# Attention scores in 64x64 quarters, router logits for two steps at once, and queries loaded half a pair per step, in a fused retention and mixture-of-experts kernel

## The chip, the cores and the metric

The kernel runs on one core of one Trainium2 chip. The time is device time in microseconds (us) of one execution on that core; of several runs the median counts, lower is better. A profile is taken from a run of its own, so its times belong to that one execution.

## What is computed

The reference has two stages. The first is a retention recurrence for 4 batches, 8 heads, 768 tokens and a head size of 64; the second routes each of the 3072 resulting rows to the best of 8 experts.

```python
gamma = 1.0 - 2.0 ** (-5.0 - np.arange(H, dtype=np.float32))
scale = 1.0 / np.sqrt(D)
for t in range(S):
    state = gamma[None, :, None, None] * state + np.einsum('bhd,bhe->bhde', k[:, :, t], v[:, :, t])
    y[:, :, t] = scale * np.einsum('bhd,bhde->bhe', q[:, :, t], state)
...
x = np.ascontiguousarray(attn_out.transpose(0, 2, 1, 3)).reshape(B * S, H * D)
...
logits = x @ w_gate
expert_idx = np.argmax(logits, axis=1)
...
    h = np.maximum(x_sorted[lo:hi] @ w1[e], 0.0)
    y_sorted[lo:hi] = h @ w2[e]
...
return (gate_w[:, None] * y).astype(np.float32)
```

`gate_w` is the softmax of the logits at the chosen expert. Everything is float32; x is 3072 x 512, w1 512 x 1024 and w2 1024 x 512 per expert.

## The kernel before

**Stages.** The attention comes first, in 12 steps, then the experts: 256 early tokens of expert 0, then all eight experts in a Strassen-like scheme of halves and quarters (from L1171 on), which is most of the time. The change is in the attention only.

**The steps.** The 768 tokens are cut into six chunks of 128. A step `s` does one chunk for two of the four batches; `where[s]` names the pair of chunks `m`, the pair of batches `b1` and the parity `e`. Steps 0, 1 are the two chunks of the first pair for the first two batches, steps 2, 3 the same for the other two batches, and so on. Both chunks of a pair share one load of `q` (token pairs interleaved), so `q` belongs to even steps and serves the odd step behind it; `k` and `v` are loaded for each step. The decay factors are folded into `q` and `v` on load, so that a step is made of plain products.

**What a step does,** in the names of the profile, for each of its two batches `b`:

- `load` (L588): L594 brings `q` (512 KB, 4 buffers), L598 `k` or `v` (256 KB, 8 buffers), all issued by SP on one DMA queue.
- `scale_q` (L601, row L606) and `scale_v` (L609, row L611) multiply by the decays, mostly on POOL, and give `qs` and `vs`.
- `turn_q` (L622) and `turn_k` (L632) transpose on PE (both row L617, `trq` and `trk`) into a PSUM bank each, which ACT copies to `qT` and `kT` (L636).
- `scores` (L642, matmul L649): per pair of heads two products of 64 x 128 keys and 64 x 128 queries, in two banks of the group `sc`; DVE multiplies by the causal mask (`am`, L653).
- `with_state` (L665, L672): y from the state so far. `next_state` (L675, L685): `new` = k v, added to the state on DVE.
- `within` (L693, L703): y from the masked scores; ACT copies the result to `xT` (2 buffers).
- `logits` (L726, L731) multiplies `xT` of the step before by the router's weights (`parts`), ACT copies that to `lgT`; `logits_of` (L737) transposes it back (L740, named `parts` too), and DVE reduces it to `lg` (L741).
- `to_rows` (L710, L714) turns `xT` of the step before on DVE into `xg` (3 buffers); `store` (L717, L721) has SP write it to `x_d` in four transfers.

PSUM has 4 banks for `sc` (scores, `trq`, `parts`), 2 for `tr` (`trk`, `new`) and 2 for `y`.

**Routing.** `place` (L747) runs after steps 5 and 9 and after the end. It finds each row's expert, counts (`ohs` L765 on DVE, `rk` L783 on PE) and sets where each row goes; it is cut into pieces, which the table `WHEN` (L896) drops into places of the steps behind. The first 256 rows of expert 0 are gathered for the early layer, `hp`, that follows step 11.

**What sets the order.** Each engine does its instructions in the order in which the code writes them: from L864 on the order of PE, ACT, POOL, DVE and SP is written by hand. The loop over steps (L902 to L977) writes, for a step s: the loads of step s + 3 (v is left off near the end), the scaling of `q` and `v` on POOL, scores, y from the state, logits of step s - 1, the turn of the next keys, the logits' transposes, the turn of the next queries if s is odd, the rows and the store of step s - 1, `new`, and `within`. SP is one line too: a load or store waits for everything before it on SP, and a store waits for its rows. SP gets the store of step 5 late, in step 7, between that step's loads of k and v. Step 8's `to_rows` needs the `xg` buffer that step 5's rows leave. The functions follow.

Of the kernel before, what the change touches and what calls it, by code (L numbers as in the profile page):

```python
# [21 lines left out]
P = 128  # L22
# [31 lines left out]
def kernel(  # L54
# [513 lines left out]
    with ExitStack() as actx:  # L568
# [32 lines left out]
        def scale_q(s, b, by=nc.gpsimd, parts=1):  # L601
            got = raw.pop(("q", s, b))
            qs = raw["qs", s, b] = att.tile([P, 2, H, D], F32, tag="qs", name="qs")
            for part in (ts(i, H // parts) for i in range(parts)):
                for e in range(2):
                    by.tensor_tensor(out=qs[:, e, part, :], in0=got[:, part, ts(e, D)], op=ALU.mult,  # L606
                                     in1=inner(dec[:, ts(2 * where[s][0] + e, H)][:, part], D))
# [24 lines left out]
        def turn_k(s, b):  # L632
            kT = att.tile([P, HP, P], F32, tag="kT", name="kT")
            tr = pairs_of("tr", 2, "trk")
            heads_first(raw["k", s, b], tr)
            nc.scalar.copy(out=kT, in_=tr)  # L636
            front[s, b] = kT
# [4 lines left out]
        def scores(s, b):  # L642
            kT, qT = front.pop((s, b)), q_of(s, b)
            sc = [pairs_of("sc", 4, "sc") for _ in range(2)]
            am = [att.tile([P, HP, P], F32, tag=f"am{j}", name=f"am{j}") for j in range(2)]
            for a in range(HP):
                for j in range(2):
                    r = ts(j, D)
                    nc.tensor.matmul(sc[j][:, a, :], lhsT=kT[r, a, :], rhs=qT[r, a, :], start=True, stop=True)  # L649

            def mask():
                for j in range(2):
                    nc.vector.tensor_tensor(out=am[j], in0=sc[j], in1=middle(causal[:, :], HP), op=ALU.mult)  # L653

            return am, mask
# [70 lines left out]
        def logits(s):  # L726
            bank = ps("sc", 4, "parts")
            parts = bank[:, 0 : 2 * P]
            m = P // DT
            for dt in range(DT):  # L730
                nc.tensor.matmul(parts[ts(dt, m), :], lhsT=wg[:, dt, :], start=True, stop=True,  # L731
                                 rhs=x[s][:, dt, :, :].rearrange("p b t -> p (b t)"))
            lgT = att.tile([P, 2 * P], F32, tag="lgT", name="lgT", bufs=1)
            nc.scalar.copy(out=lgT, in_=parts)
            return lgT, bank

        def logits_of(s, lgT, bank):  # L737
            tr = bank[:, 2 * P : 4 * P].rearrange("p (b t) -> p b t", b=2)
            for b in range(2):
                nc.tensor.transpose(tr[:, b, :], lgT[:, ts(b, P)], ident)  # L740
            return lambda: nc.vector.tensor_reduce(  # L741
                lg[:, 2 * s : 2 * s + 2, :], tr.rearrange("p b (a e) -> p b e a", a=DT)[:, :, 0:E, :], axis=AX.X,
                op=ALU.add)
# [124 lines left out]
        scale_q(0, 0, nc.vector, 2)  # L868
# [33 lines left out]
        for s in range(STEPS):  # L902
            if s + 3 < STEPS:
                if s % 2:
                    load_all("q", s + 3)
                load_all("k", s + 3)
                if s == 7:
                    store(5)
                if s + 4 < STEPS:
                    load_all("v", s + 3)  # L910
            if s % 2 and s + 1 < STEPS:
                scale_q(s + 1, 1)
            if s + 2 < STEPS:
                for b in range(2):
                    scale_v(s + 1, b)
            if s % 2 == 0 and s + 2 < STEPS:
                scale_q(s + 2, 0)
            if s in (1, 2):
                nc.gpsimd.memset(xs2[s % 2], 0.0)
            if s:  # L920
                am = [scores(s, b) for b in range(2)]
                am[0][1]()
                step(s, "m")
                if s + 2 != STEPS:
                    am[1][1]()
            y = outputs()
            if s + 1 == STEPS:
                logit = logits(s - 1)
                rows_in_order()
# [12 lines left out]
            if s:  # L942
                if s + 1 < STEPS:
                    logit = logits(s - 1)
                    ahead()
                reduce = logits_of(s - 1, *logit)
                step(s, "p")
                if s + 2 == STEPS:
                    am[1][1]()
                    for b in range(2):  # L950
                        scale_v(s + 1, b)
                if s + 1 < STEPS:
                    ahead_q()
                to_rows(s - 1)
# [14 lines left out]
            next_state(s)  # L969
            step(s, "b")  # L970
# [4 lines left out]
            if s == 0:  # L975
                ahead()
# [9 lines left out]
        def within_early(f):  # L986
            nonlocal ne, arm, src, far
            if f == 1:
                logits_of(STEPS - 1, *logit)()
# [21 lines left out]
        for f in range(FT):  # L1011
            layer1(EARLY, xTa, wa[0], hTa, f, (("sc", 4),), lambda: within_early(f))
            if f == 0:
                logit = logits(STEPS - 1)
# [282 lines left out]
```

## Time and profile before

| | |
|---|---|
| median of 3 runs | 439.09 us (439.05 to 440.54) |
| the profiled execution's own time | 442.87 us |
| its span in the profile | 441.2 us |
| instructions in the profile | 9756 |
| PE busy | 420.9 us (95% of the span), 3595 matmuls |
| DVE / POOL / ACT busy | 244.9 / 252.6 / 130.4 us |
| attention | 0 to about 118.7 us, where the row `hp` of the early layer starts |
| moved by DMA in all | 85.39 MB, mean 194 GB/s |

The span runs from the first to the last instruction that the profiler saw, so it is a little shorter than the time. In the profile's rows, PE is the matmul part of the tensor engine and PEld its weight loads, which overlap; DVE is the vector engine, ACT the scalar engine, POOL the GpSimd engine, SP the engine that only issues transfers, and SPq its DMA queue. A row of the timeline is the start, the busy time, the engine and the source line, what is written and read with its shape, how many instructions stand in it, and in brackets how long the first one waited and for what. A row of the chain of waits is start, length, and who held the chain. Forty digits in a row are the span in forty equal slices, each digit the busy tenths. A row of the windows is the stretch, its length, busy time and count for PE, PEld, DVE, ACT and POOL, then the granted PE clock, the DMA engines' mean busy share and their GB/s. A row of one line's instructions gives the least, middle and greatest nanoseconds of one and the stretch in which they lie.

### The profile page before, as it was taken

How to read it: one execution, taken by the hardware profiler on the slowest of the kernel's cores; microseconds unless marked ns; L12 is line 12 of the kernel's file. 1: busy time of each engine (PE TensorE's matmuls, PEld its weight loads, DVE VectorE, ACT ScalarE, POOL GpSimd, SP SyncE). 2: the span in 40 equal slices, each digit the busy share in tenths (PEclk: the TensorE clock that was granted, in tenths of full speed). 3: DMA queues.
4: the chain of work that ended last, by engine and by line, in shares of the span. 5: the costliest groups of instructions: out<-in, count | busy, mean ns of one | idle time of the engine just before them, and what ended most of it. 6: DMA issues, size and time to landing. Idle time of an engine off the chain costs nothing.

```text
span 441.2 us, 9756 instructions
## 1 busy us (share of the span) xinstructions
PE 420.9 (95%) x3595; PEld 385.7 (87%) x3595; DVE 244.9 (56%) x565; ACT 130.4 (30%) x293; POOL 252.6 (57%) x212
## 2 busy tenths in 40 slices
PE   7889989999999999999999999999999999999990
PEld 4778877887788858999999999999999999999680
DVE  4445577769779960444672674377178247544320
ACT  2355452553521212201322222031223213303330
POOL 4477254553338352989329926983992892585051
PEclk9999999999999999999999999999999999999997
DMA  9989999999991497643955694496599449222222
GB/s 196 237 199 205 237 203 218 219 229 222 285 337 45 127 402 244 216 149 94 385 131 161 245 277 95 125 377 158 165 316 244 116 142 348 57 84 52 49 74 75
DMA packets 122123, 85.39 MB, mean 194 GB/s; under 512 B 56970, under 2 KB 106122, under 8 KB 122000
## 3 DMA queue, kind: packets, MB, share of 16 engines
q1 hardware_dynamic: 116736, 71.34, 59.5%
q0 software_dynamic: 5120, 12.60, 8.6%
q8 instruction: 49, 0.80, 0.8%
q14 instruction: 74, 0.61, 0.5%
q10 hardware_dynamic: 144, 0.05, 0.1%
HBM read 60.88 MB, written 14.68 MB: 171 GB/s over the span
## 4 chain that ended last, share of the span: by engine, by line
PE 82%; DMA 5%; SPq 4%; DVE 4%; issue 2%; ACT 1%; another core or an unknown queue 0%; POOLq 0%; DVEq 0%; ACTq 0%
PE p L333 51%; PE p L233 6%; DMA k<-in_k_dram 4%; PE p L246 4%; PE hp L233 3%; PE sc L649 3%; PE y L703 3%; SPq L598 3%; PE p L474 2%; PE new L685 2%; PE trq L617 2%; PE y L672 1%; PE trk L617 1%; DVE xTa L217 1%; PE parts L731 1%
## 5 line engine op out<-in xcount | busy, mean ns | idle before, releaser
L337 DVE TENSOR_TENSOR q<-p,q 128x196 f32<-128x196 f32 (+5 forms) x72 | 24.0, 352 | 41.8 <-PE p L333 35.1
L653 DVE TENSOR_TENSOR am<-sc,causal 128x512 f32<-128x512 f32 x48 | 30.0, 683 | 20.5 <-PE sc L649 20.4
L522 POOL DMA_INDIRECT out_dram<-o,dst x26 | 25.9, 996 | 26.4 <-ACT o L1167 19.5
L611 POOL TENSOR_TENSOR vs<-v,dec 128x512 f32<-128x512 f32 x23 | 24.6, 1084 | 26.5 <-DMA v<-in_v_dram 25.0
L174 POOL DMA_INDIRECT xs<-x_d,src x28 | 30.8, 1099 | 13.9 <-issue 9.8
L333 PE MATMUL p<-t,w1t 128*128 128x196 f32 (+5 forms) x192 | 35.9, 330 | 0.0
L333 PE MATMUL p<-t,s 128*128 128x196 f32 (+5 forms) x192 | 35.8, 329 | 0.0
L333 PE MATMUL p<-g,w2t 128*128 128x216 f32 (+5 forms) x192 | 35.3, 337 | 0.0
L337 DVE TENSOR_TENSOR yT<-p,q 128x216 f32<-128x216 f32 (+5 forms) x36 | 13.0, 374 | 39.5 <-PE p L333 31.0
L333 PE MATMUL p<-g,z 128*128 128x196 f32 (+4 forms) x192 | 33.6, 328 | 0.0
L333 PEld LDWEIGHTS p<-g,w2t 128*128 128x128 f32 x192 | 33.4, 190 | 0.0
L606 POOL TENSOR_TENSOR qs<-q,dec 128x512 f32<-128x512 f32 x22 | 22.4, 1044 | 19.1 <-DMA q<-in_q_dram 16.7
L337 DVE TENSOR_TENSOR hT<-p,q 128x196 f32<-128x196 f32 (+5 forms) x72 | 24.2, 351 | 16.0 <-PE p L333 15.6
L333 PE MATMUL p<-hT,w2t 128*128 128x196 f32 (+4 forms) x192 | 32.6, 328 | 0.0
L333 PEld LDWEIGHTS p<-t,w1t 128*128 128x128 f32 x192 | 32.4, 190 | 0.2 <-DVE q L337 0.2
L333 PEld LDWEIGHTS p<-t,s 128*128 128x128 f32 x192 | 32.5, 190 | 0.0
L1251 POOL COPY turn_of<-t 128x1 f32<-128x1 f32 x6 | 1.1, 184 | 54.5 <-DVE t L318 54.5
L333 PEld LDWEIGHTS p<-g,z 128*128 128x128 f32 x192 | 31.9, 190 | 0.0
L333 PEld LDWEIGHTS p<-hT,w2t 128*128 128x128 f32 x192 | 31.7, 190 | 0.0
L649 PE MATMUL sc<-qT,kT 64*128 64x128 f32 x384 | 24.9, 279 | 2.3 <-ACT kT L636 2.3
L649 PEld LDWEIGHTS sc<-qT,kT 64*128 64x128 f32 x384 | 22.4, 188 | 4.4 <-ACT kT L636 3.0
L703 PE MATMUL y<-am,vs 128*64 128x128 f32 x384 | 24.1, 274 | 0.5 <-issue 0.3
(231 smaller groups left out, 886.1 us busy)
## 6 DMA issues: line engine op xcount, KB each, us to landing
w1t<-in_moe_w_dram SPq DMA_DIRECT2D x7, 2048.0 KB
w2t<-in_moe_w_dram SPq DMA_DIRECT2D x7, 2048.0 KB
k<-in_k_dram SPq DMA_DIRECT2D x24, 256.0 KB
v<-in_v_dram SPq DMA_DIRECT2D x24, 256.0 KB
x_d<-xg SPq DMA_DIRECT2D x48, 128.0 KB
xs<-xs SPq DMA_DIRECT2D x96, 64.0 KB
o<-o SPq DMA_DIRECT2D x96, 64.0 KB
q<-in_q_dram SPq DMA_DIRECT2D x11, 512.0 KB
```

What stands on the lines that cost most here:

```text
L174: nc.gpsimd.indirect_dma_start(out=xs[:, t, :], out_offset=None, in_=x_d[0:rows, :], in_offset=bass.IndirectOffsetOnAxis(ap=idx[:, t : t + ...
L233: nc.tensor.matmul(hp, lhsT=w1t[:, 0, dt, ts(f, P)], rhs=xT[:, dt, n0:n], start=(dt == 0), stop=(dt == DT - 1))
L246: nc.tensor.matmul(y[j * z : j * z + m, 0:c], lhsT=hT[:, f, t * P + r0 : t * P + r0 + m], rhs=w2t[:, 0, f, ts(j, c)], start=(i == 0), stop ...
L333: nc.tensor.matmul(columns(y, c), lhsT=a, rhs=b, start=start and i == 0, stop=i + 1 == len(terms), skip_group_check=True)
L337: nc.vector.tensor_tensor(out=to, in0=y, in1=plus, op=ALU.add)
L522: done = nc.gpsimd.indirect_dma_start(out=out[:, :], out_offset=bass.IndirectOffsetOnAxis(ap=idx[:, t : t + 1], axis=0), in_=o[:, t, :], i ...
L606: by.tensor_tensor(out=qs[:, e, part, :], in0=got[:, part, ts(e, D)], op=ALU.mult, in1=inner(dec[:, ts(2 * where[s][0] + e, H)][:, part], D))
L611: by.tensor_tensor(out=vs, in0=raw.pop(("v", s, b)), op=ALU.mult, in1=inner(dec[:, ts(NC + 2 * where[s][0] + where[s][2], H)], D))
L617: nc.tensor.transpose(tr[:, a, :], src[:, 2 * a : 2 * a + 2, :].rearrange("p h d -> p (h d)"), ident)
L649: nc.tensor.matmul(sc[j][:, a, :], lhsT=kT[r, a, :], rhs=qT[r, a, :], start=True, stop=True)
L653: nc.vector.tensor_tensor(out=am[j], in0=sc[j], in1=middle(causal[:, :], HP), op=ALU.mult)
L703: nc.tensor.matmul(place_of(y, b, a, j), lhsT=vs[:, 2 * a + j, :], rhs=am[b][0][j][:, a, :], start=alone, stop=True, skip_group_check=True)
```

## The change

Six things change, all in the attention.

1. `scores` makes each product of 64 x 128 keys as two of 64 x 64 keys, each to one half of the partitions of the bank. A batch's step has 16 matmuls in place of 8; the profile counts each float32 matmul as two rows, so a step of two batches goes from 32 rows to 64.
2. `logits` takes a list of steps. Step 1 does step 0's; from step 3 on an odd step does the logits of the two steps before it, in one bank, with one copy, four transposes into the same bank and one reduction over both; an even step does none. Step 11's own logits stay alone.
3. `turn_k` of the second batch goes to a bank of `sc` in place of `tr` when it is called for the turn of an odd step's keys, which is done in an even step.
4. SP loads `k` first in each step, then one of the two `q` of the next even step (the first in even steps, the second in odd ones), then `v`. Among the first loads, `wg` and the `v` of step 1 move behind.
5. POOL scales accordingly; in step 1 the second `q` of step 2 is scaled half by DVE and half by POOL, and one `v` of step 1 by DVE. The two memsets of `xs2` are in steps 2 and 3 in place of 1 and 2.
6. Step 1's keys are turned ahead of step 0's `within` instead of behind it, and `to_rows` of step 0 is written ahead of those scalings in step 1.

The first place is SP's line around the store of step 5 (`x_d`, the fifth row), before:

```order
L598 DMA k<-in_k_dram 128x8x64 x2
L598 DMA v<-in_v_dram 128x8x64 x2
L594 DMA q<-in_q_dram 128x8x128 x2
L598 DMA k<-in_k_dram 128x8x64 x2
L721 DMA x_d<-xg 32x8x128 x4
L598 DMA v<-in_v_dram 128x8x64 x2
```

And after the change:

```order
L598 DMA k<-in_k_dram 128x8x64 x2
L594 DMA q<-in_q_dram 128x8x128
L598 DMA v<-in_v_dram 128x8x64 x2
L598 DMA k<-in_k_dram 128x8x64 x2
L594 DMA q<-in_q_dram 128x8x128
L723 DMA x_d<-xg 32x8x128 x4
L598 DMA v<-in_v_dram 128x8x64 x2
```

One `q` now stands ahead of `v` in the step before and one behind `k` in step 7; the transfers ahead of the store are the same set.

The second place is PE in step 11, the last step (`tot` belongs to the routing), before:

```order
L649 MATMUL sc<-qT,kT 128x128 x16
L731 MATMUL parts<-xT,wg 32x256 x4
L672 MATMUL y<-qT,state_1863 64x128 x16
L740 MATMUL parts<-ident,lgT 128x128 x2
L841 LDWEIGHTS ones_b
L841 MATMUL tot<-acc,ones_b 128x2
```

And after:

```order
L650 MATMUL sc<-qT,kT 64x128 x32
L734 MATMUL parts<-xT,wg 32x256 x8
L674 MATMUL y<-qT,state_2013 64x128 x16
L744 MATMUL parts<-ident,lgT 128x128 x4
L845 LDWEIGHTS ones_b
L845 MATMUL tot<-acc,ones_b 128x2
```

The order counts each matmul once and names the shape of its output, 128 x 128 before and 64 x 128 now; the scores' rows double. So do the logits' rows, since they hold steps 9 and 10.

The third place is PE in step 2, an even one (the y at the top ends `within` of step 1), before:

```order
L703 MATMUL y<-am_356,vs 64x128
L649 MATMUL sc<-qT,kT 128x128 x16
L731 MATMUL parts<-xT,wg 32x256 x4
L617 MATMUL trk<-ident,k 128x128 x8
L740 MATMUL parts<-ident,lgT 128x128 x2
L685 MATMUL new<-vs,k 64x64 x16
```

And after, with the start of `within` as the last row:

```order
L705 MATMUL y<-am_368,vs 64x128
L650 MATMUL sc<-qT,kT 64x128 x32
L617 MATMUL trk<-ident,k 128x128 x8
L687 MATMUL new<-vs,k 64x64 x16
L705 MATMUL y<-am_535,vs 64x128
```

Both rows of `parts` have left the step, and the rest keeps its order.

The diff, cut to its core:

```diff
         def turn_k(s, b):
             kT = att.tile([P, HP, P], F32, tag="kT", name="kT")
-            tr = pairs_of("tr", 2, "trk")
+            tr = pairs_of("sc", 4, "trk") if s % 2 and b else pairs_of("tr", 2, "trk")
...
             for a in range(HP):
-                for j in range(2):
-                    r = ts(j, D)
-                    nc.tensor.matmul(sc[j][:, a, :], lhsT=kT[r, a, :], rhs=qT[r, a, :], start=True, stop=True)
+                for c in range(2):
+                    for j in range(2):
+                        r = ts(j, D)
+                        nc.tensor.matmul(sc[j][ts(c, D), a, :], lhsT=kT[r, a, ts(c, D)], rhs=qT[r, a, :],
+                                         start=True, stop=True)
...
-        def logits(s):
+        def logits(steps):
+            n = 2 * len(steps)
             bank = ps("sc", 4, "parts")
...
+            for i, s in enumerate(steps):
+                for dt in range(DT):
+                    nc.tensor.matmul(bank[ts(dt, m), ts(i, 2 * P)], lhsT=wg[:, dt, :], start=True, stop=True,
+                                     rhs=x[s][:, dt, :, :].rearrange("p b t -> p (b t)"))
+            lgT = att.tile([P, 4 * P], F32, tag="lgT", name="lgT", bufs=1)
+            nc.scalar.copy(out=lgT[:, 0 : n * P], in_=bank[:, 0 : n * P])
...
-        nc.sync.dma_start(wg[:, :, 0:E], w_gate.rearrange("(dt p) e -> p dt e", p=P))
         load_all("v", 0)
         load_all("k", 1)
-        load_all("v", 1)
+        nc.sync.dma_start(wg[:, :, 0:E], w_gate.rearrange("(dt p) e -> p dt e", p=P))
         load("q", 2, 0)
+        load_all("k", 2)
+        load("v", 1, 0)
         load("q", 2, 1)
-        load_all("k", 2)
+        load("v", 1, 1)
...
             if s + 3 < STEPS:
-                if s % 2:
-                    load_all("q", s + 3)
                 load_all("k", s + 3)
+                n = s + 4 - s % 2
+                if n < STEPS:
+                    load("q", n, s % 2)
                 if s == 7:
                     store(5)
...
                 if s + 1 < STEPS:
-                    logit = logits(s - 1)
+                    if s % 2:
+                        logit = logits([s - 1] if s == 1 else [s - 2, s - 1])
                     ahead()
-                reduce = logits_of(s - 1, *logit)
+                reduce = logits_of(*logit) if s % 2 else lambda: None
...
+                if s == 1:
+                    to_rows(0)
+                    scale_q(2, 1, (nc.vector, nc.gpsimd))
+                    scale_v(1, 1)
+                    for b in range(2):
+                        scale_v(2, b)
...
             next_state(s)
+            if s == 0:
+                ahead()
             step(s, "b")
...
             within(s, y, am, early_rows if s + 1 == STEPS else lambda: None)
-            if s == 0:
-                ahead()
```

More of the change, by code (lines that the diff above doesn't have):

```diff
@@ L599, in load, with scale_q @@
             raw[nm, s, b] = to
-        def scale_q(s, b, by=nc.gpsimd, parts=1):
+        def scale_q(s, b, by=(nc.gpsimd, nc.gpsimd), parts=1):
             got = raw.pop(("q", s, b))
@@ L605, in scale_q @@
                 for e in range(2):
-                    by.tensor_tensor(out=qs[:, e, part, :], in0=got[:, part, ts(e, D)], op=ALU.mult,
+                    by[e].tensor_tensor(out=qs[:, e, part, :], in0=got[:, part, ts(e, D)], op=ALU.mult,
                                      in1=inner(dec[:, ts(2 * where[s][0] + e, H)][:, part], D))
@@ L724, with logits_of @@
         early, wa = [], []
-        def logits(s):
+        def logits(steps):
+            n = 2 * len(steps)
             bank = ps("sc", 4, "parts")
-            parts = bank[:, 0 : 2 * P]
             m = P // DT
[L730 to L739, printed above, removed]
+            for i, s in enumerate(steps):
[4 more added lines that the diff above has]
+            nc.scalar.copy(out=lgT[:, 0 : n * P], in_=bank[:, 0 : n * P])
+            return steps, lgT, bank
+        def logits_of(steps, lgT, bank):
+            n = 2 * len(steps)
+            tr = bank[:, 0 : n * P].rearrange("p (b t) -> p b t", b=n)
+            for b in range(n):
                 nc.tensor.transpose(tr[:, b, :], lgT[:, ts(b, P)], ident)
             return lambda: nc.vector.tensor_reduce(
-                lg[:, 2 * s : 2 * s + 2, :], tr.rearrange("p b (a e) -> p b e a", a=DT)[:, :, 0:E, :], axis=AX.X,
-                op=ALU.add)
+                lg[:, 2 * steps[0] : 2 * steps[0] + n, :], tr.rearrange("p b (a e) -> p b e a", a=DT)[:, :, 0:E, :],
+                axis=AX.X, op=ALU.add)
         MOST_T = 2 * max(b - a for a, b in zip(NEXT, NEXT[1:]))
@@ L867 @@
         hTa = keep.tile([P, FT, EARLY], F32, tag="hTa", name="hTa")
-        scale_q(0, 0, nc.vector, 2)
+        scale_q(0, 0, (nc.vector, nc.vector), 2)
         scale_q(0, 1)
@@ L910 @@
                     load_all("v", s + 3)
-            if s % 2 and s + 1 < STEPS:
-                scale_q(s + 1, 1)
-            if s + 2 < STEPS:
+            if s == 0:
+                scale_q(2, 0)
+            elif 1 < s < STEPS - 2:
+                if s % 2:
+                    scale_q(s + 1, 1)
                 for b in range(2):
                     scale_v(s + 1, b)
-            if s % 2 == 0 and s + 2 < STEPS:
-                scale_q(s + 2, 0)
-            if s in (1, 2):
+                if s % 2 == 0:
+                    scale_q(s + 2, 0)
+            if s in (2, 3):
                 nc.gpsimd.memset(xs2[s % 2], 0.0)
@@ L925 @@
                     am[1][1]()
+                if s == 1:
+                    scale_v(1, 0, nc.vector)
             y = outputs()
             if s + 1 == STEPS:
-                logit = logits(s - 1)
+                logit = logits([s - 2, s - 1])
                 rows_in_order()
@@ L943 @@
                 if s + 1 < STEPS:
-                    logit = logits(s - 1)
+                    if s % 2:
+                        logit = logits([s - 1] if s == 1 else [s - 2, s - 1])
                     ahead()
-                reduce = logits_of(s - 1, *logit)
+                reduce = logits_of(*logit) if s % 2 else lambda: None
                 step(s, "p")
@@ L951 @@
                         scale_v(s + 1, b)
+                if s == 1:
+                    to_rows(0)
[3 more added lines that the diff above has]
+                        scale_v(2, b)
                 if s + 1 < STEPS:
                     ahead_q()
-                to_rows(s - 1)
+                if s > 1:
+                    to_rows(s - 1)
                 reduce()
@@ L969 @@
             next_state(s)
+            if s == 0:
+                ahead()
             step(s, "b")
@@ L988, in within_early @@
             if f == 1:
-                logits_of(STEPS - 1, *logit)()
+                logits_of(*logit)()
                 next(rest)
@@ L1013 @@
             if f == 0:
-                logit = logits(STEPS - 1)
+                logit = logits([STEPS - 1])
         hs = [att.tile([P, FH * P], F32, tag="k", name="he", bufs=8) for _ in range(4)]
```

## The prediction

> **What bounds the kernel now.** I began with the page, asked for the chain of waits over the first 180 us, then read the timelines of SP, DVE, PE and POOL there, and last the windows of the DMA queue. The change touches only the attention stage, which runs to about 118.7 us; the experts behind it stay word for word the same.
>
> From the page: the span, the busy share of the 16 DMA engines in 40 slices of 11 us, and the traffic of instruction fetches (packets, MB, share).
>
> ```profile
> span 441.2 us, 9756 instructions
> ...
> DMA  9989999999991497643955694496599449222222
> ...
> q8 instruction: 49, 0.80, 0.8%
> ```
>
> The DMA engines are full for eleven slices, exactly the attention stage. So PE at 95% is only half of the story: in this stage the loads may be the bound. The chain of waits decides (start, length, what).
>
> ```profile
> 52.18 6.97 DMA k<-in_k_dram
> ...
> 71.59 6.98 DMA k<-in_k_dram
> ...
> 94.36 2.58 DMA x_d<-xg
> ...
> 97.02 0.53 DVE xg L714
> ...
> 101.22 0.23 DVE ohs L765
> ...
> 101.50 0.19 PE rk L783
> ...
> 108.86 0.09 DVE am L653
> ...
> 110.19 1.52 PE y L703 x22
> 111.72 1.99 PE sc L649 x32
> ```
>
> It goes through a load of k twice (steps 5 and 7), then, in step 9, through the store of step 5's rows: with three `xg` buffers, step 8's rows can be turned only when step 5's have left. From there DVE carries it (routing, `ohs`), PE's `rk` waits for that, and DVE again lets the second half of step 10's y go at 110.19. Everything up to 97.02 is therefore timed by the DMA queue, if the queue waits for nobody. Whether it does is seen by comparing when rows are ready (DVE, steps 1 and 4) with when SP issues their stores (same steps).
>
> ```profile
> 33.03 1.29 DVE L714 STREAM_TRANSPOSE xg<-xT 128x512 f32<-128x512 f32 x2
> ...
> 57.25 1.29 DVE L714 STREAM_TRANSPOSE xg<-xT 128x512 f32<-128x512 f32 x2
> ```
>
> ```profile
> 45.14 4.04 SPq L721 DMA_DIRECT2D x_d<-xg  x4
> ...
> 77.34 3.52 SPq L721 DMA_DIRECT2D x_d<-xg  x4
> ```
>
> Ready at 34.3 and 58.5, issued at 45.1 and 77.3: SP is 11 to 19 us behind, because the loads in front of it drain slowly. Nothing that PE, DVE or ACT does faster moves this queue. That is my central reading: **the attention stage is a stream of loads and stores with a fixed number of bytes, and the last event that it gates is 97.02.**
>
> **What the change does, part by part.**
>
> *The order of the loads.* SP's rows show k, half a pair of q, v per step instead of a whole pair of q ahead of every second k. Ahead of the store of step 5 stands the same set of transfers before and after, so the gate at 97.02 doesn't move by this: 0. Inside the stream, the even step's k comes one 512 KB load earlier and the second q takes its place. PE's waits for k in steps 1 and 5 (in brackets):
>
> ```profile
> 22.99 0.66 PE L617 MATMUL trk<-ident,k 128*128 128x128 f32 x4 [0.99 <-DMA k<-in_k_dram]
> 24.06 0.66 PE L617 MATMUL trk<-ident,k 128*128 128x128 f32 x4 [0.41 <-DMA k<-in_k_dram]
> ...
> 58.26 0.66 PE L617 MATMUL trk<-ident,k 128*128 128x128 f32 x4 [0.94 <-DMA k<-in_k_dram]
> 59.20 0.66 PE L617 MATMUL trk<-ident,k 128*128 128x128 f32 x4 [0.28 <-DMA k<-in_k_dram]
> ```
>
> ```profile
> 53.93 4.05 POOL L606 TENSOR_TENSOR qs<-q,dec 128x512 f32<-128x512 f32 x4 [3.65 <-DMA q<-in_q_dram]
> ```
>
> These 2.6 us go, but what is late next is the second q: it lands where the second k landed, POOL then scales it (two of 4.05/4 = 1.01 us, 2.0 in all), and the last four transposes of it follow (0.5): PE is past the turns 2.5 us after the landing. Before, it was: four transposes of k, the logits' two, sixteen of q, 0.47 + 0.22 + 1.91 = 2.6 us by the rows below. So the wait changes its name and keeps its size: 0 in steps 5 and 7. On POOL the waiting `qs` has only the two `vs` of the same step behind it, whose v lands later still.
>
> *The scores, logits, second keys and first turn on PE.* PE's rows of step 3 (start, busy, group, wait in brackets), and behind them its scores of step 1 and its `new` of step 4:
>
> ```profile
> 36.35 2.06 PE L649 MATMUL sc<-qT,kT 64*128 64x128 f32 x32
> 38.34 1.10 PE L672 MATMUL y<-qT,state 64*64 64x128 f32 x32
> 39.37 0.64 PE L731 MATMUL parts<-xT,wg 128*32 128x256 f32 x8
> 39.94 1.09 PE L617 MATMUL trk<-ident,k 128*128 128x128 f32 x8
> 40.87 0.38 PE L740 MATMUL parts<-ident,lgT 128*128 128x128 f32 x2
> 41.09 1.91 PE L617 MATMUL trq<-ident,qs 128*128 128x128 f32 x16
> ```
>
> ```profile
> 18.34 2.06 PE L649 MATMUL sc<-qT,kT 64*128 64x128 f32 x32 [0.85 <-ACT kT L636]
> ...
> 50.83 1.15 PE L685 MATMUL new<-vs,k 128*64 128x64 f32 x32 [0.17 <-ACT kT L636]
> ```
>
> Scores take 38.34 - 36.35 = 1.99 us in 32 rows. In quarters they are 64 rows in the shape of the y beside them, which takes 1.03 for 32: at most 2 x 1.03 = 2.06, a change of +0.07. The entry into a new shape is in that figure twice and would be paid once; estimated at up to a quarter of a y, it makes the other end 2.06 - 0.26 - 1.99 = -0.19. I take this end, rounded to -0.2, since a stream of one shape pays the entry once. Logits, odd steps: twice the parts, +0.28 (half of 0.57, were it all entry) to +0.57, I take +0.45, and two more transposes, +0.22. Even steps lose both, -0.79. The second key in a scores' bank takes `new`'s 0.17 wait away; the earlier turn of step 1's keys takes 0.85. Together an odd step costs PE 0.45 + 0.22 - 0.2 = +0.47 and an even one -0.79 - 0.17 - 0.2 = -1.16: -0.7 a pair, -2.8 over four pairs, and with the waits of step 1 (0.85 + 0.99 + 0.41 = 2.25) some 5.0 us less for PE up to step 9. **All of it lies ahead of the gate**: PE would reach `rk` earlier and wait there, where it now waits a quarter of a microsecond. It is worth 0 there, and it is what the first rival collects.
>
> The Trainium skill, TensorEngine Tiling (Array Packing), under Theoretical Speedup, promises up to fourfold throughput for four 64x64 tiles, so twice that of two tiles of 64x128; by it the scores would take 1.0 us. The rows say otherwise, since each quarter streams the same 128 columns and there are twice as many; by that section step 11 below would be 0.8 us shorter and the sum +1.2 instead of +2.0.
>
> *Behind the gate.* The reduction of the logits stands on DVE between the turned rows and the routing:
>
> ```profile
> 98.25 0.19 DVE L741 TENSOR_REDUCE lg<-parts 128x16 f32<-128x64 f32 x1
> ```
>
> It now has two steps' input: 0 to +0.19, I take +0.1. Step 10 ends by DVE (110.19), so its missing logits give nothing. Step 11 is PE's own, from 111.72 on, and is an odd one: +0.45 + 0.22 - 0.2 = +0.47.
>
> *What the quarters add to the DMA queue.* They double the rows of L649, 384 more matmuls and 384 more weight loads.
>
> ```profile
> L649 PEld LDWEIGHTS sc<-qT,kT x384: 182/188/188, 7.9 to 113.3; 64*128 64x128 f32 x192
> L649 PE MATMUL sc<-qT,kT x384: 272/272/373, 7.9 to 113.4; 64*128 64x128 f32 x192
> ```
>
> The page has 49 instruction packets of 0.80 MB / 49 = 16 KB, one per 9756/49 = 199 instructions. They run on the same 16 engines. Windows of the first steps (columns end with clock, DMA share, GB/s):
>
> ```profile
> 17.00:22.00 5.00, 4.15 (x77) 3.14 (x75) 2.47 (x5) 1.74 (x4) 2.61 (x3) 1.00 1.08 253
> ...
> 28.40:29.50 1.10, 1.10 (x24) 0.93 (x18) 0.10 (x1) 0.59 (x1) 0.56 (x1) 1.00 0.28 61
> ...
> 30.40:31.40 1.00, 1.00 (x20) 0.90 (x18) 0.77 (x2) 0.33 (x1) 0.49 (x1) 1.00 0.48 84
> ```
>
> ```profile
> 18.00:36.00 18.00, 16.09 (x272) 13.98 (x274) 9.10 (x16) 8.14 (x16) 11.58 (x11) 1.00 0.97 220
> 36.00:54.00 18.00, 17.83 (x322) 15.53 (x320) 9.22 (x16) 8.96 (x18) 8.31 (x9) 1.00 0.95 208
> 54.00:72.00 18.00, 16.60 (x305) 14.29 (x303) 13.22 (x31) 8.01 (x16) 9.13 (x13) 1.00 0.97 212
> 72.00:90.00 18.00, 17.13 (x280) 14.11 (x278) 12.26 (x28) 8.69 (x16) 9.14 (x8) 1.00 1.05 228
> ```
>
> The queue has holes in which most engines are empty though SP has work for them. What makes a hole no view names; one engine held by a 16 KB packet, while SP can't issue past it, would do it, and that is my reading. Price: an undisturbed stretch has share 1.08, the four long windows 0.985 on average, so 72 x 0.095/1.08 = 6.3 us are lost there; they hold about 2550 instructions, 2550/199 = 12.8 fetches: 0.5 us each. Bounds: 0 (hidden), and 0.81 + 0.56 = 1.4 if the two dips shown are one fetch. Steps 0 to 8 add 9 x 64 = 576 rows, 2.9 fetches ahead of the gate: +1.45 (0 to +4.0).
>
> The Trainium skill, Runtime: NRT & Kernel Launch, under Instruction fetch mechanics, has 16 KiB blocks of 256 instructions, which would make it 2.25 fetches and +1.1; that agrees with the 16 KB of the row. It also calls the cost of a block mostly hidden, which is the second rival.
>
> **Sum**: 0 (order) + 0 (PE ahead of the gate) + 1.45 + 0.1 + 0.47 = +2.0 us. The profiled execution took 442.87 (span 441.2), so 444.9 (span 443.2). The timed runs' median, 439.09, lies 3.8 lower; I carry the same difference over: **441.1 us**. A measurement of this kernel can tell about 0.5%, 2.2 us: 436.9 and 441.3 are the borders of "same".
>
> **The rivals.**
> 1. *The queue isn't the bound in the timed runs.* They are 3.8 us shorter than the profiled one; if profiling slows the queue by more than the waits it causes now (2.6 in steps 1 and 5, and less than 1 more), PE is the bound there and its 5.0 us count, less the 0.6 behind the gate: 439.1 - 4.4 = 434.7 where all counts, 437 where half does. For it: the waits for DMA are small. Against: SP's 11 to 19 us. Chance 0.25 (0.16 faster, 0.09 same).
> 2. *Fetches are hidden, and nothing else moves*: 439.09 + 0.57 = 439.7. For it: PE's rows show no wait for instructions of any size. Against: the holes. Chance 0.15.
> 3. *POOL becomes the bound*, on the slower side: in steps 3, 5 and 7 it does the second q, in order, behind the `vs` of the step and a memset in step 3. If it starts more than a microsecond after the landing, PE's turns of q are late by that, some 1 us in each of three steps on top of the sum: 444. Against: POOL's 3.65 idle ahead of `qs` in step 5. Chance 0.08.
>
> The forecast has 0.52, from 439.7 to 443.6, about half on either side of 441.3: 0.25 same, 0.27 slower. Together: faster 0.16, same 0.25 + 0.09 + 0.15 = 0.49, slower 0.27 + 0.08 = 0.35. The range of 436.5 to 443.3 leaves out rival 1 where all of it counts, rival 3 and the last of the fetches' bounds.
>
> **What would show it.** In the changed kernel's profile: DMA slices still full to 110 us; `trq` of the second batch waiting for POOL's `qs` in steps 5 and 7 in place of `trk` for k; `rk` of step 9 waiting for `ohs` by 1.5 us or more; `xg` of step 8 ending its wait on a store at 98 to 99; three or four more instruction packets; step 11 half a microsecond longer. I am wrong if `xg` of step 8 no longer waits for a store, or waits for one that lands before 96.5, or if `rk` starts before 100.

## The result and the profile after

| | before | changed | ratio, 95% interval |
|---|---|---|---|
| first measurement | 439.92 us (6 runs, 439.05 to 441.78) | 446.11 us (6 runs, 442.82 to 447.21) | 1.0118 (1.0087 to 1.015) |
| repeated on another chip | 439.39 us | 444.78 us (6 runs, 440.91 to 447.14) | 1.0126 (1.0082 to 1.017) |

The ratio here and below is one of means. The changed kernel is 1.2% slower, some 5 us; forecast were 2.0 us more, 441.1 us in all, in a range that ended at 443.3. Its page says of the span, the granted clock in 40 slices, and the instruction fetches:

```profile
span 445.5 us, 10495 instructions
...
PEclk9989999899999999999999999999999999999997
...
q8 instruction: 52, 0.85, 0.8%
```

Three more fetches, as forecast. New is the second 8 in the clock's row, the eighth slice, 78 to 89 us. The timeline there, all engines:

```profile
78.75 1.78 PE L617 MATMUL trq<-ident,qs 128*128 128x128 f32 x12
78.78 3.63 POOL L606 TENSOR_TENSOR qs<-q,dec 128x512 f32<-128x512 f32 x2 [3.34 <-DMA q<-in_q_dram]
...
79.23 2.27 DVE L820 TENSOR_TENSOR val<-at,told 128x1600 bf16<-128x1600 f32 x1
...
82.46 0.66 PE L617 MATMUL trq<-ident,qs 128*128 128x128 f32 x4 [1.92 <-POOL qs L606]
83.05 1.25 PE L687 MATMUL new<-vs,k 128*64 128x64 f32 x32
84.08 3.52 PE L705 MATMUL y<-am,vs 128*64 128x128 f32 x32
```

This is step 7. The second `q` has landed; POOL scales it in 3.63 us where two of 1.01 were forecast, and DVE's `val`, a piece of the routing, lies in that time. The second scaling ends at 82.41, 0.9 us behind `val`. PE waits 1.92 for the last four transposes. Then comes y, which takes 3.52 us and not 1.92 though it waits for nobody. The windows say why (third column from the end: granted clock):

```profile
82.00:83.90 1.90, 1.44 (x32) 1.27 (x34) 0.00 (x0) 0.64 (x1) 1.90 (x3) 1.00 1.04 234
83.90:87.30 3.40, 3.40 (x43) 3.40 (x38) 2.32 (x11) 0.59 (x1) 0.51 (x1) 0.51 0.80 209
87.30:90.00 2.70, 2.70 (x94) 2.47 (x95) 1.31 (x3) 1.16 (x2) 0.77 (x1) 0.99 1.38 222
```

For 3.4 us PE has half its clock. Step 1 has the same, from 25.9 to 29.3. The two profiles of before have no such stretch in the attention.

The execution of before that the prediction read took longer in the attention than usual: its repeat has a span of 438.3 in place of 441.2, and `hp` starts at 115.89 in place of 118.72. So the two kernels are compared by the two profiles of the repeat, which come from one chip. The repeat of before, step 7 and the start of 8 and 9:

```profile
71.51 2.06 PE L649 MATMUL sc<-qT,kT 64*128 64x128 f32 x32
...
76.26 1.91 PE L617 MATMUL trq<-ident,qs 128*128 128x128 f32 x16
78.10 1.15 PE L685 MATMUL new<-vs,k 128*64 128x64 f32 x32
79.08 1.92 PE L703 MATMUL y<-am,vs 128*64 128x128 f32 x32
80.93 2.06 PE L649 MATMUL sc<-qT,kT 64*128 64x128 f32 x32
82.91 1.10 PE L672 MATMUL y<-qT,state 64*64 64x128 f32 x32
...
89.51 1.72 PE L649 MATMUL sc<-qT,kT 64*128 64x128 f32 x26
```

The same stretch in the repeat of the changed kernel:

```profile
71.47 1.98 PE L650 MATMUL sc<-qT,kT 64*64 64x128 f32 x64
73.27 1.05 PE L674 MATMUL y<-qT,state 64*64 64x128 f32 x32
...
76.62 1.04 PE L617 MATMUL trq<-ident,qs 128*128 128x128 f32 x8
77.07 3.62 POOL L606 TENSOR_TENSOR qs<-q,dec 128x512 f32<-128x512 f32 x2 [3.18 <-DMA q<-in_q_dram]
78.17 0.66 PE L617 MATMUL trq<-ident,qs 128*128 128x128 f32 x4 [0.51 <-POOL qs L606]
80.75 0.97 PE L617 MATMUL trq<-ident,qs 128*128 128x128 f32 x4 [1.93 <-POOL qs L606]
81.66 1.98 PE L687 MATMUL new<-vs,k 128*64 128x64 f32 x32
83.42 2.38 PE L705 MATMUL y<-am,vs 128*64 128x128 f32 x32
85.73 1.98 PE L650 MATMUL sc<-qT,kT 64*64 64x128 f32 x64
...
93.05 1.98 PE L650 MATMUL sc<-qT,kT 64*64 64x128 f32 x64
```

Both start step 7 at 71.5; step 8 starts at 80.93 and at 85.73. **In this pair of profiles one step holds the whole loss: 14.26 us in place of 9.42, 4.84 more.** By the rows: 0.40 up to `trq` (an odd step's logits), 3.20 from there to `new` (the waits of 0.51 and 1.93, 0.31 in the slower last transposes, and a rest of 0.45), 0.78 in `new` and 0.46 in y. So the waits are 2.4 us and the halved clock is 0.31 + 0.78 + 0.46 = 1.55. Step 8 gives 1.26 back (7.32 in place of 8.58), which leaves 3.54 in step 9. Step 11, from its scores to `hp`, in the repeat of before:

```profile
108.67 2.06 PE L649 MATMUL sc<-qT,kT 64*128 64x128 f32 x32
...
115.89 1.35 PE L233 MATMUL hp<-xTa,w1t 128*128 128x256 f32 x5
```

And in that of the changed kernel:

```profile
112.24 1.98 PE L650 MATMUL sc<-qT,kT 64*64 64x128 f32 x64
...
119.84 1.35 PE L233 MATMUL hp<-xTa,w1t 128*128 128x256 f32 x5
```

7.60 in place of 7.22, and `hp` starts 3.95 later. The spans differ by 442.1 - 438.3 = 3.8: behind the attention nothing is added.

### The profile page after: what moved, and what is told of

Its sections match the earlier page's. It is cut to its first block, busy times and chain, and to the rows that moved or that the text cites. A ratio compares the mean times of both kernels' runs of the same rounds, so it can differ in the third digit from the quotient of the medians.

```text
span 445.5 us, 10495 instructions
## 1 busy us (share of the span) xinstructions
PE 421.7 (95%) x3979; PEld 387.2 (87%) x3979; DVE 244.8 (55%) x562; ACT 129.8 (29%) x288; POOL 251.2 (56%) x210
## 4 chain that ended last, share of the span: by engine, by line
PE 76%; DMA 9%; issue 4%; POOL 3%; DVE 3%; SPq 2%; ACT 1%; POOLq 1%; DVEq 0%; ACTq 0%
PE p L333 49%; PE p L233 6%; DMA q<-in_q_dram 6%; PE p L246 4%; PE y L705 3%; PE hp L233 3%; PE sc L650 3%; PE new L687 2%; POOL qs L606 2%; DMA w1t<-in_moe_w_dram 2%; PE trk L617 1%; DVE xTa L217 1%; SPq L598 1%; PE trq L617 1%; PE y L674 1%
## 5 line engine op out<-in xcount | busy, mean ns | idle before, releaser
L522 POOL DMA_INDIRECT out_dram<-o,dst x26 | 25.9, 996 | 26.3 <-ACT o L1185 19.7
L606 POOL TENSOR_TENSOR qs<-q,dec 128x512 f32<-128x512 f32 x21 | 23.6, 1143 | 24.4 <-DMA q<-in_q_dram 20.7
L611 POOL TENSOR_TENSOR vs<-v,dec 128x512 f32<-128x512 f32 x22 | 22.6, 1045 | 22.7 <-DMA v<-in_v_dram 21.4
L705 PE MATMUL y<-am,vs 128*64 128x128 f32 x384 | 26.1, 287 | 1.3 <-issue 0.8
L650 PE MATMUL sc<-qT,kT 64*64 64x128 f32 x768 | 24.0, 272 | 1.4 <-ACT kT L636 1.4
L705 PEld LDWEIGHTS y<-am,vs 128*64 128x64 f32 x384 | 22.8, 146 | 2.6 <-issue 1.5
```

Source lines behind the costliest of these rows:

```text
L522: done = nc.gpsimd.indirect_dma_start(out=out[:, :], out_offset=bass.IndirectOffsetOnAxis(ap=idx[:, t : t + 1], axis=0), in_=o[:, t, :], i ...
L606: by[e].tensor_tensor(out=qs[:, e, part, :], in0=got[:, part, ts(e, D)], op=ALU.mult, in1=inner(dec[:, ts(2 * where[s][0] + e, H)][:, part ...
L611: by.tensor_tensor(out=vs, in0=raw.pop(("v", s, b)), op=ALU.mult, in1=inner(dec[:, ts(NC + 2 * where[s][0] + where[s][2], H)], D))
L650: nc.tensor.matmul(sc[j][ts(c, D), a, :], lhsT=kT[r, a, ts(c, D)], rhs=qT[r, a, :], start=True, stop=True)
L705: nc.tensor.matmul(place_of(y, b, a, j), lhsT=vs[:, 2 * a + j, :], rhs=am[b][0][j][:, a, :], start=alone, stop=True, skip_group_check=True)
```

## The experiments

Theory 1: PE waits for POOL's scaling of the second q, the wait brings a halved clock, and the lateness reaches the end. Theory 2, the prediction's: the doubled rows of the scores cost through their fetches. Each ratio is against the kernel before, run beside it.

**The loads of before in the changed kernel, and the new loads alone in the kernel before.** The edit of the first is the second's with the signs turned; of the second's, the loop's loads and the start of POOL's scaling:

```diff
-                if s % 2:
-                    load_all("q", s + 3)
                 load_all("k", s + 3)
+                n = s + 4 - s % 2
+                if n < STEPS:
+                    load("q", n, s % 2)
...
-            if s % 2 and s + 1 < STEPS:
-                scale_q(s + 1, 1)
-            if s + 2 < STEPS:
+            if s == 0:
+                scale_q(2, 0)
+            elif 1 < s < STEPS - 2:
+                if s % 2:
+                    scale_q(s + 1, 1)
```

> The changed kernel with its load order and its scaling taken back to those of before (quarters, logits in twos, the second key's bank and step 1's early turn stay). Theory 1 (PE's idle time behind POOL's scaling of the second q, and the halved clock that follows it, are the loss): both are gone, sc of step 8 starts at 84 or earlier, no stretch with a granted clock of 0.5, rk of step 9 at 101.5, time 0.5 to 1 us above before, 440.5 (439 to 441.5). Theory 2 (the doubled rows of the scores cost through their fetches, or on PE): the time stays near the changed kernel's 446.

> The kernel before with the load order, the scaling and the early rows of step 1 of the changed kernel and nothing else. Theory 1: the second q still waits for POOL in steps 1 and 7, PE idles 1.5 us or more and the granted clock falls to 0.5 at least once: 444 to 447. Theory 2: without quarters no further fetches, so the time of before, 439.9, give or take 1.

Ratios 1.0036 (1.0004 to 1.0068) and 1.0080 (1.0057 to 1.0102): two thirds of the loss are the load order's, with no quarter in the kernel, as theory 1 has it; theory 2 falls. In the profile of the new loads alone no stretch had half the clock and PE's longest wait for POOL was 0.78 us, so that part of its expectation isn't borne out by that execution; over its 12 runs the mean granted clock was 0.993, before's 0.995. The first's mean clock was 0.991, though its one profile has no stretch at half clock either; what makes its 0.36% isn't settled.

**`val` out of POOL's way.**

```diff
-        WHEN = {5: "abc", 6: "b", 7: "ab", 8: "pp", 9: "ac", 10: "mpp"}
+        WHEN = {5: "abc", 6: "bb", 7: "b", 8: "pp", 9: "ac", 10: "mpp"}
```

> The changed kernel with one piece of the routing (val on DVE, 2.3 us) moved from step 7's logits to the end of step 6, where DVE is idle from 72.0 to 74.3. Theory 1: POOL's second qs of step 7 takes 2.05 us in place of 3.63, the last trq starts at 80.9 in place of 82.46, PE idles less than a microsecond there, y of step 7 takes 1.9 in place of 3.5 and sc of step 8 starts at 84.3 in place of 87.5; the time falls by 2.5 to 3.5 us, to 443. Theory 2: the same 446.

1.0067 (1.0045 to 1.0088). In its timeline:

```profile
77.51 2.05 POOL L606 TENSOR_TENSOR qs<-q,dec 128x512 f32<-128x512 f32 x2 [1.28 <-DMA q<-in_q_dram]
78.61 0.66 PE L617 MATMUL trq<-ident,qs 128*128 128x128 f32 x4 [0.54 <-POOL qs L606]
...
79.61 0.66 PE L617 MATMUL trq<-ident,qs 128*128 128x128 f32 x4 [0.35 <-POOL qs L606]
80.20 1.15 PE L687 MATMUL new<-vs,k 128*64 128x64 f32 x32
81.18 1.92 PE L705 MATMUL y<-am,vs 128*64 128x128 f32 x32
```

POOL takes 2.05 and PE waits 0.9 in place of 2.4; from the landing of q at 77.51 to `new` at 80.20 are 2.7 us; `new` and y have their old durations. 0.5% of the 1.2% are gone.

**PE's waits filled.** First with transposes that PE had done already, repeated (20 in step 1, 16 in step 7), then with idle matmuls of 512 columns, ahead of the transposes that wait; the second's edit:

```diff
+                    if (s, b, e) in ((2, 1, 0), (8, 1, 1)):
+                        for _ in range(2):
+                            nc.tensor.matmul(trs[e].rearrange("p a t -> p (a t)"), lhsT=idle[:, 0:P], rhs=idle,
+                                             start=True, stop=True)
                     heads_first(qs[:, e, :, :], trs[e], range(i * HP // parts, (i + 1) * HP // parts))
```

> The changed kernel with PE's waits for the second q in steps 1 and 7 filled by repeats of transposes that it has already done (20 and 16 more, 2.2 and 1.75 us of work; nothing that is stored changes). The waits for POOL stay as they are. If the idle time is what halves the clock: new of step 1 takes 1.1 in place of 2.0, y of step 7 takes 1.9 in place of 3.5, sc of step 8 starts at 85.9 in place of 87.5, and the time falls by 1.5 to 2.5 us, to 444. If the halved clock has another cause (the load on the engines, a fixed moment): it stays, and the time is 446 or a little more.

> The changed kernel with two idle matmuls of 512 columns each on PE ahead of the turn of the second q in step 1 and of its last four transposes in step 7, in place of the repeated transposes of the first attempt. The waits for POOL stay. If the idle time causes the halved clock: clock 0.992 or more in place of 0.987, 2 to 3 us less, a ratio of 1.005 to 1.008; new of step 1 takes 1.15 in place of 1.7 to 2.0. If not: ratio and clock as they were, 1.012 and 0.987.

1.0203 (1.0172 to 1.0233) and 1.0129 (1.0099 to 1.0158): no gain in time, which misses both expectations. The second's mean clock did come back, to 0.993; the first's was 0.990. Where the fill met the wait the clock stayed whole: `new` of step 1 took 1.15 in both, where the changed kernel's two profiles have 1.98 and 1.68. But in the first, PE waited 3.17 us in step 5 for POOL instead and the clock halved there (62 to 66 us); its early layer started at 120.77, 2.4 sooner than in the changed kernel's first profile, and the experts then lost more in waits which that profile has not (us in all, times, the longest; `issue` is a wait for nothing that the profile shows):

```profile
PE p L333 <- issue: 2.5, 2, 1.5
PE p L333 <- POOL s L286: 1.2, 1, 1.2
```

The changed kernel's repeat has one such wait, of 1.3 us. Why is open. In the second, DVE's `val` met the first half of the scaling, PE waited one group earlier than the fill, and the fill came on top, at half clock:

```profile
79.40 0.66 PE L617 MATMUL trq<-ident,qs 128*128 128x128 f32 x4 [2.21 <-POOL qs L606]
79.89 3.01 PE L630 MATMUL trq<-idle 128*128 128x512 f32 x4
82.70 1.06 PE L617 MATMUL trq<-ident,qs 128*128 128x128 f32 x4
```

**Quarters alone, and the rest without them.** The first is the diff of `scores` on the kernel before; the second has the logits in twos, the second key's bank and the early turn of step 1's keys.

> The kernel before with the scores in quarters and nothing else. The prediction's price of the doubled rows (3 to 4 more fetches that hold the queue, half a microsecond each) gives 1.2 to 2 us more, a ratio of 1.003 to 1.005, and the store of step 5 lands later by as much. If PE's 0.1 to 0.2 us a step are only added to its waits for the loads: a ratio of 0.998 to 1.002, and the mean granted clock as before (0.995).

> The run with the loads of before once more, without its quarters: logits in twos, the second key's bank and step 1's early turn, on the kernel before. If what it lost (a ratio of 1.0036) comes from PE being early, which lengthens its wait for k in step 1 and with it the chance of a halved clock: the ratio stays above 1.002 and the mean clock below 0.993. If it came from the quarters: ratio 1.000 or below, clock 0.995.

1.0001 (0.9975 to 1.0027) and 1.0012 (0.9996 to 1.0028). The quarters cost nothing that can be measured, with all 52 fetches on their page. The second saves PE work and gains nothing. The ratio above 1.002 that was expected didn't come, but its mean clock fell to 0.991 as expected, and the profile shows the cause that was expected, a wait for k and the clock behind it:

```profile
22.71 0.66 PE L617 MATMUL trk<-ident,k 128*128 128x128 f32 x4 [1.65 <-DMA k<-in_k_dram]
```

```profile
24.00:26.00 2.00, 2.00 (x13) 2.00 (x12) 0.22 (x1) 0.94 (x3) 1.13 (x3) 0.60 1.07 239
26.00:28.00 2.00, 2.00 (x11) 1.81 (x9) 0.00 (x0) 1.54 (x3) 2.00 (x2) 0.55 1.18 234
```

**Both kernels again.** No edit.

> The changed kernel once more. Theory 1: a ratio of 1.010 to 1.015; the mean granted clock over all runs at 0.985 to 0.990 against 0.995 of before, so 2 to 4 us of PE's clock lost beyond it; in the profile each stretch of 0.5 lies within 4 us behind a wait of PE for POOL's qs of 1.5 us or more. If the halved clock was an accident of one execution: clock 0.995 and the ratio below 1.008.

> The kernel before once more, one look. Its execution on record had a span of 441.2 with the early layer at 118.7 us, its other runs end 3 to 4 us sooner. If the difference is in the attention's stream of loads: the store of step 5 lands at 93 to 95 in place of 96.9, the early layer starts at 115 to 117, and the stretch behind it is 320.6 to 322.4 as in the other profiles. If it lies in the experts: the early layer at 118 to 119.

1.0126 (1.0082 to 1.017), with a mean clock of 0.987 against 0.994 of before: the halved clock is no accident of one execution. Before's early layer started at 115.89, so its first profile had lost its time in the attention.

**Is step 1's halved clock part of the loss?** The run without quarters, with two idle matmuls ahead of the turn of step 2's keys (in step 1), or with step 1's keys turned late as in before:

```diff
+            if (s, b) == (2, 0):
+                for _ in range(2):
+                    nc.tensor.matmul(tr.rearrange("p a t -> p (a t)"), lhsT=idle[:, 0:P], rhs=idle, start=True, stop=True)
             heads_first(raw["k", s, b], tr)
```

> The run without quarters on the loads of before, and two idle matmuls of 512 columns (0.85 us each) on PE ahead of step 1's turn of the next keys, into the bank that the turn then overwrites: they fill the wait of 1.65 us for k and change no result. If PE's idle time causes the halved clock: no stretch of 0.5 behind step 1, the mean clock back from 0.991 to 0.994 or more, and the time 1 to 1.3 us below that run: a ratio of 0.997 to 0.999. If not: clock 0.991 and a ratio of 1.001 or more.

> The run without quarters on the loads of before, with step 1's keys turned behind step 0's products again, so that only the logits in twos and the second key's bank are left of the change. PE then waits 0.85 for kT and 1.0 for k in two pieces in place of 1.65 in one. If one long wait is what matters: clock 0.994 or more and a ratio of 0.997 to 1.000. If it is the sum of the waits: clock 0.991 and 1.001.

1.0022 (0.9998 to 1.0047) and 1.0002 (0.9976 to 1.0028). The clock did as expected, 0.994 in both, but the time didn't fall below that of before: a halved clock in step 1 costs nothing at the end that these intervals show. The starts of the scores show where it goes (us, one profile each):

| | step 2 | step 5 | step 6 | step 8 | `hp` |
|---|---|---|---|---|---|
| before, repeat | 29.4 | 53.8 | 63.6 | 80.9 | 115.9 |
| without quarters | 30.8 | 53.6 | 64.1 | 81.0 | 115.7 |
| the same, filled | 29.5 | 52.5 | 64.6 | 82.2 | 116.8 |

By step 6 the lead of the filled run is gone: it is a microsecond earlier at step 5 and waits there for k, the other comes when k has landed. Filled:

```profile
57.49 0.66 PE L617 MATMUL trk<-ident,k 128*128 128x128 f32 x4 [0.89 <-DMA k<-in_k_dram]
58.53 0.66 PE L617 MATMUL trk<-ident,k 128*128 128x128 f32 x4 [0.39 <-DMA k<-in_k_dram]
```

**Clock put right in the changed kernel.** `val` early, and step 1's wait filled.

> The changed kernel with val at the end of step 6 and step 1's wait filled, so that the clock has no reason left to fall: clock 0.994 or more. What then remains above before is the price of the waits alone that the load order makes: by the difference of time and lost clock in the runs so far 1.5 to 2.5 us, a ratio of 1.003 to 1.006. If the clock were the only loss of the change: a ratio of 0.998 to 1.000.

1.0079 (1.0051 to 1.0107), clock 0.994. So with a whole clock 0.8% remain, somewhat more than expected, and the clock isn't the only loss.

**q ahead of k in odd steps.**

```diff
+                n = s + 4 - s % 2
+                if n < STEPS and s % 2:
+                    load("q", n, 1)
                 load_all("k", s + 3)
-                n = s + 4 - s % 2
-                if n < STEPS:
-                    load("q", n, s % 2)
+                if n < STEPS and s % 2 == 0:
+                    load("q", n, 0)
```

> The changed kernel with one swap in its loop of loads: in odd steps the half pair of q is issued ahead of k in place of behind it, so that k lands last again and POOL has its 2 us for the second q while k is still on its way. If what is left of the loss (a ratio of 1.007 to 1.008 with val moved) is POOL's work standing between the last landing and PE: steps 5 and 7 lose less than half a microsecond against before, no halved clock behind step 7, a ratio of 1.000 to 1.004. If it is the queue itself that is slower with half pairs: still 1.007 or more, the store of step 5 landing 1.5 us or more later than before.

1.0033 (1.0007 to 1.0058), inside what was expected if POOL's work behind the last landing is the loss. Step 7 has no wait and takes 10.5 us in place of 14.26. That steps 5 and 7 would lose less than half a microsecond against before didn't come: step 7 has 1.1 us more than the repeat of before, and step 5 4.6 more (51.95 to 66.36), of which 1.8 are its earlier start. So what is left has an example in step 5, where PE was early and waited for k, and the clock halved behind the wait:

```profile
57.70 0.66 PE L617 MATMUL trk<-ident,k 128*128 128x128 f32 x4 [1.91 <-DMA k<-in_k_dram]
...
59.85 3.33 PE L617 MATMUL trq<-ident,qs 128*128 128x128 f32 x16
```

**A wait and a work of 2 us in step 7 of the kernel before.** Both are meant to make PE some 2 us late; only one leaves it idle. The second has the loop over `n` too (`idle2` is a second tile like `idle`):

```diff
+            if (s, b) == (8, 0):
+                for n in (4, 4, 2):
+                    nc.tensor.matmul(trs[0][:, 0:n, :], lhsT=idle2[:, 0:P], rhs=idle2[:, 0 : n * P], start=True, stop=True)
+                nc.tensor.matmul(trs[0][:, 0, :], lhsT=idle[:, 0:P], rhs=idle[:, 0:P], start=True, stop=True)
...
+            if s == 7:
+                for _ in range(7):
+                    nc.gpsimd.memset(idle, 1.2345678)
```

> The kernel before, with PE made to wait in step 7: ahead of the turn of the next queries one small matmul needs a tile that POOL fills in seven memsets behind its scaling of q, some 2 us later than PE arrives. Nothing that is stored changes. If a wait of 2 us halves the clock behind it and PE's time in step 7 counts: a stretch of 0.5 behind 78 us, the mean clock 0.990 to 0.991 in place of 0.9945, and 3 to 4 us more, a ratio of 1.007 to 1.009. By the prediction's reading, in which PE's time ahead of the store of step 5 is worth nothing: a ratio of 1.000 to 1.003.

> The same as the run with the idle wait, with 2.1 us of idle matmuls on PE in front of the small one, so that PE is late by as much but busy all the while. If the idle time halves the clock: no stretch of 0.5, the mean clock 0.994, and 1.5 us less than the run with the wait, a ratio of 1.003 to 1.006. If the lateness alone costs: the same time as that run.

1.0127 (1.0083 to 1.0171) with the wait, more than expected, and 1.0056 (1.0034 to 1.0078) with the work, as expected; mean clocks of 0.992 and 0.995. With the wait:

```profile
79.95 0.80 PE L629 MATMUL trq<-idle 128*128 128x128 f32 x2 [2.48 <-POOL idle L919]
80.54 3.21 PE L619 MATMUL trq<-ident,qs 128*128 128x128 f32 x16
```

With the work:

```profile
76.37 2.31 PE L630 MATMUL trq<-idle 128*128 128x512 f32 x6
78.52 0.39 PE L631 MATMUL trq<-idle 128*128 128x128 f32 x2
78.74 1.91 PE L619 MATMUL trq<-ident,qs 128*128 128x128 f32 x16
```

The sixteen transposes take 3.21 behind the wait and 1.91 behind the work. The wait alone, put into the kernel before, makes a loss of the changed kernel's size. Between the two lies 0.7%, 3.1 us. In the two profiles the turn of q starts 80.54 - 78.74 = 1.8 later with the wait, and then takes 1.3 longer, at half clock; the end of the attention is 3.1 later (`hp` at 120.9 and 117.8). Of the 1.8, 1.1 come from ahead of the wait, by what the loads did in that execution (PE came to the wait at 79.95 - 2.48 = 77.47, to the work at 76.37); 0.3 are the wait's greater length (2.48, and 78.52 - 76.37 = 2.15 of work); and 0.4 are the small matmul, at half clock already (0.59 in place of 0.22). So the halved clock is 1.3 + 0.4 = 1.7. How the 3.1 of all the runs divide isn't known.

## Why the prediction was wrong

- **"The wait changes its name and keeps its size: 0 in steps 5 and 7."** This step failed, in step 7. Its term is the 2.5 us from the landing of the second q to the end of PE's turns: there it was 4.3 in the first profile (78.78 to 83.05) and 4.6 in the repeat (77.07 to 81.66). Against the repeat of before, where PE waited for no load in this step, that is 3.2 us more from `trq` to `new`. The two scalings of 1.01 each didn't stay 2.0: they ran while DVE ran `val`, and the second took 2.6 and ended 0.9 behind `val`. Moving `val` brought 2.05 back, and 2.7 from the landing. In step 5, where no `val` runs, the term held: 2.7 us in the first profile (59.46 to 62.14). The Trainium skill, SBUF — State Buffer, under SBUF: two separate sides, has a port pair that DVE and GpSimd lock for a whole instruction; the 3.63 against 2.05 agrees. The runs show the overlap and its cost, not the lock itself. The prediction's own third rival had the engine right and a chance of 0.08; but its condition, a start of POOL more than a microsecond behind the landing, didn't come, and in place of 1 us in each of three steps it was 2.4 us of waits in one.
- **The clock.** Nothing in the prediction asked what an idle PE costs afterwards. It is 1.55 us in step 7. The Trainium skill, TensorE: Matmul & The Clock Gate, under HAM oscillation, warns of idle gaps of more than about 3.4 us: the length of the halved stretches is that (83.9 to 87.3), but here shorter waits were enough to start one. In the attention of the 17 profiles, from 10 us on, all seven waits of 1.91 us and more were followed by half the clock. Of the six from 1.54 to 1.84 us two were (1.63 and 1.65) and four weren't (1.54, another 1.63, 1.71 and 1.84), so in between the length of the wait alone doesn't decide.
- **"All of it lies ahead of the gate. It is worth 0."** True of time saved: the logits in twos with the second key's bank have a ratio of 1.0002, and the quarters 1.0001. Taken the other way it is wrong: 2.3 us of work put into step 7 cost 0.56%, some 2.5 us. The slack is the quarter of a microsecond that the prediction quoted at `rk`; lateness beyond it passes. The prediction counted the gate as a bound on both sides. It would be wrong, it said, if `xg` of step 8 no longer waited for a store. So it is in the changed kernel's first profile, where `rk` waits for nobody either:

```profile
98.42 1.29 DVE L716 STREAM_TRANSPOSE xg<-xT 128x512 f32<-128x512 f32 x2
...
103.89 0.20 PE L787 MATMUL rk<-ohs,before 128*128 128x64 bf16 x1
```

The repeat and the two runs with 2 us in step 7 have the same: PE had become the bound. The store of step 5 wasn't later: SP starts it at 87.83 in the repeat, and at 88.25 in that of before. So in this pair the stream of loads itself isn't slower.

- **The fetches**, +1.45: 0, by the quarters alone (-0.25% to +0.27%, so at most 1.2 us). The holes in the queue are there in before, but three more fetches add no time that can be measured. The "mostly hidden" of the Trainium skill, Runtime: NRT & Kernel Launch, under Instruction fetch mechanics, which stood beside the price, agrees with this run.
- **The sizes of PE's own work were right.** Scores 73.27 - 71.47 = 1.80 in place of 1.98 (forecast -0.2); an even step -1.26 (forecast -1.16); step 11 +0.38 (forecast +0.47); the reduction 0.29 us against 0.19 (forecast +0.1). Four tiles of 64x64 aren't twice as fast as two of 64x128 here.
- **The carry-over.** Taking 3.8 us off the profiled execution was harmless for the ratio, but that execution made the loads look more binding than they usually are: in the repeat of before, k of step 7 keeps PE waiting no more. The prediction also counted eleven full slices of the DMA engines, exactly the attention; its row has twelve, up to 132 us, past the attention's end.
- **The direction.** That the forecast said slower is mostly luck: of its +2.0, the 1.45 of the fetches isn't there, and only the half microsecond behind the gate came as said.

In the changed kernel's first profile `hp` waits another 1.45 us for its weights, whose load took 8.69 us from issue. The repeat hasn't got it; its cause is open. What makes the remaining third of a per cent of the run with q ahead of k isn't settled either.

## What to carry to other kernels

A stage timed by transfers forgives an engine that is early, not one that is late by more than the slack at the gate: price both directions. When the order of loads changes, ask what work stands between the last landing and the engine that waits, on which engine, and what else runs beside it then. A wait on PE of some 2 us can cost 1.5 to 1.7 us more in the clock behind it, so one long wait is worse than the same work. For one long wait against several short ones only the clock shows it here (0.991 against 0.994), not the time.

## What the runs showed of the hardware

- The granted clock fell to 0.5 for 3.4 us behind waits of PE of 1.65 us (for k in step 1), 1.91, 2.4 (in two pieces) and 2.48 us, in a kernel that else kept PE busy. It isn't certain at the short end: a wait of 1.71 us for k in step 1 of the run with the loads of before left it at 1.00, and so did one of 1.84 in step 1 of the run with q ahead of k. Waits of 0.85, 1.01 and 0.41 us within step 1 of before left it at 1.00 too.
- A scaling of 128x512 on POOL, 1.04 us alone, took 2.6 us when DVE's product of 128x1600 elements (2.3 to 2.7 us) ran beside it: it ended 0.9 us behind the product, almost its own length, in both profiles of the changed kernel.
- Idle matmuls hold the clock up, but only where the wait falls; put a group too late they add their own time (two of 512 columns took 3.01 us at half clock, 1.88 at full).
